# A decode kernel of two attention and GLU layers: K transposed by VectorE in 32x32 blocks, wide matmuls over four batches, softmax merged late

## The chip, the cores and the metric

One core of one Trainium2 chip. The metric is the device time of one execution, in microseconds (us). Times are medians with their range. TensorE is the matmul engine, VectorE, ScalarE and GpSimd are the three others; in the profile they are PE, DVE, ACT and POOL, PEld is TensorE's weight load, SP the queue that issues most loads.

## The reference

Two identical layers follow one another. Each adds attention over a cache and then a gated unit to x. There is one new token per batch, so the whole work is reading the K and V caches: 4 batches x 8 kv heads x 4096 keys x 128 x 2 bytes = 33.5 MB each. Both layers read the same caches, and both kernels load them once per layer, so they are read twice: 134 MB, plus 14 MB of weights, 148.1 MB in all.

```python
B, Sq, D = 4, 1, 512
Hq, Hkv, Sk, Dh = 32, 8, 4096, 128        # 4 q heads share a kv head; F = 1792
# all inputs bf16
def attention(x, k_cache, v_cache, wq, wo):
    q = (x @ wq).reshape(B, Sq, Hq, Dh).transpose(0, 2, 1, 3)
    k = jnp.repeat(k_cache, 4, axis=1); v = jnp.repeat(v_cache, 4, axis=1)
    p = softmax(einsum("bhqd,bhkd->bhqk", q, k) * Dh ** -0.5)
    return einsum("bhqk,bhkd->bhqd", p, v).transpose(0, 2, 1, 3).reshape(B, Sq, Hq * Dh) @ wo
def glu(x, w_gate, w_up, w_down):
    return (sigmoid(x @ w_gate) * (x @ w_up)) @ w_down

x = x + attention(layernorm(x), ...);  x = x + glu(layernorm(x), ...)   # twice
```

## The kernel before

The loop runs over the 32 (batch, kv head) pairs of a layer, 64 in all. K arrives with keys on the partitions; TensorE turns it with 32 identity matmuls per pair, and VectorE and ScalarE copy the results out of PSUM. Then 32 matmuls of 4 columns give the scores, with the keys on the partitions again. So a maximum or a sum over keys must cross partitions, and GpSimd does that.

```python
def pe_transpose_fill(base, i, f, ...):        # 4 fills per pair, 8 blocks each
    fns = [lambda e: e.transpose(tps[:, bb*P:(bb+1)*P], kn_buf[s][:, j, :], ident_bf) for bb in ...]
    S.group("pe", fns, ...)
    # ... cut: the copy out of PSUM, on ScalarE for one bank of four and on VectorE for three

def pe_scores(i):                              # 32 matmuls, K stationary, 4 q columns moving
    e.matmul(S_ps[p][:, j*REP:(j+1)*REP], lhsT=kt_sb[kb][:, j, :], rhs=qT_sb[:, b, g*REP:(g+1)*REP], ...)

def dve_reduce1(i):                            # L662: maximum inside each partition
    S.inst("dve", lambda e: e.tensor_reduce(hmax_sb[p], S_ps[p]..., AX.X, ALU.max), ...)

def pool_max(i):
    S.inst("pool", lambda e: e.partition_all_reduce(gmax_sb[p][:, :], hmax_sb[p][:, :], P, RO.max), ...)   # L673
    S.inst("pool", lambda e: e.tensor_scalar_mul(negbc_sb[p][:, :], gmax_sb[p][:, :], -att_scale), ...)    # L679

def act_exps(i):                               # L689: one exponential per q head
    e.activation(pexp_sb[p][:, :, h], S_ps[p][:, bass.ds(h, NJ, step=REP)], ACTF.Exp,
                 bias=negbc_sb[p][:, h:h+1], scale=att_scale, accum_out=rowsum_sb[p][:, h:h+1])

def pool_den(i):
    S.inst("pool", lambda e: e.partition_all_reduce(den_sb[p][:, :], rowsum_sb[p][:, :], P, RO.add), ...)  # L704

def dve_final(i):                              # L714, L720
    e.reciprocal(rden_sb[p], den_sb[p]);  e.tensor_tensor(oT_sb[...], O_ps[p][:, 0:REP], rden_sb[p], ALU.mult)

for i in range(NI):                            # the order inside a layer; fills of K for i + 1 are woven in
    pe_scores(i); dve_reduce1(i); pool_max(i); act_exps(i)
    if i >= 1:
        pe_pv(i - 1, 0, half); pe_pv(i - 1, half, NJ)     # 32 matmuls, V stationary, 4 columns moving
        pool_den(i - 1); dve_final(i - 1)
# ... cut: layer norm (reciprocal root by three Newton steps), projections, GLU
```

Each load of K or V puts 32 successive keys on a partition: rows of 8 KB.

Of the kernel before, what the change touches and what calls it, by code (L numbers as in the profile page):

```python
# [5 lines left out]
dt = mybir.dt  # L6
ACTF = mybir.ActivationFunctionType
ALU = mybir.AluOpType
AX = mybir.AxisListType
RO = bass.bass_isa.ReduceOp  # L10
# [4 lines left out]
class _Token:  # L15
    __slots__ = ("sem_key", "needed", "value", "inc")

    def __init__(self, sem_key, inc=1, needed=False):
        self.sem_key = sem_key
        self.needed = needed  # L20
        self.value = None
        self.inc = inc


class _Item:
    __slots__ = ("fn", "token", "waits")

    def __init__(self, fn, token, waits):
        self.fn = fn
        self.token = token  # L30
        self.waits = waits


class _Sched:

    def __init__(self):
        self.prog = {e: [] for e in ENGINES}
        self.all_items = []
        self.last_write = {}
        self.readers = {}  # L40

    def _inst(self, eng, fn, deps, sem_key, inc, needed):
        tok = _Token(sem_key, inc=inc, needed=needed)
        waits = []
        for d in deps:
            if d is None:
                continue
            d.needed = True
            waits.append(d)
        item = _Item(fn, tok, waits)  # L50
        self.prog[eng].append(item)
        self.all_items.append(item)
        return tok

    def group(self, eng, fns, reads=(), writes=(), deps=(), sem_key=None, inc=1, needed=False):
        assert eng in ENGINES
        if sem_key is None:
            sem_key = eng
        deps = [d for d in deps if d is not None]
        for k in reads:  # L60
            w = self.last_write.get(k)
            if w is not None:
                deps.append(w)
        for k in writes:
            w = self.last_write.get(k)
            if w is not None:
                deps.append(w)
            deps.extend(self.readers.get(k, ()))
        tok = None
        first = True  # L70
        for fn in fns:
            tok = self._inst(eng, fn, deps if first else (), sem_key, inc, needed)
            first = False
        for k in writes:
            self.last_write[k] = tok
            self.readers[k] = []
        for k in reads:
            self.readers.setdefault(k, []).append(tok)
        return tok

    def inst(self, eng, fn, reads=(), writes=(), deps=()):
        return self.group(eng, [fn], reads=reads, writes=writes, deps=deps)

    def dma(self, eng, fn, sem_key, reads=(), writes=(), deps=()):
        return self.group(eng, [fn], reads=reads, writes=writes, deps=deps, sem_key=sem_key, inc=16, needed=True)

    def assign_values(self):
        counts = {}
        for it in self.all_items:
            t = it.token  # L90
            if t.needed:
                c = counts.get(t.sem_key, 0) + t.inc
                counts[t.sem_key] = c
                t.value = c
        return counts

    def emit(self, eng, eng_obj, sems):
        waited = {}
        for it in self.prog[eng]:
            need = {}  # L100
            for w in it.waits:
                if w.value > need.get(w.sem_key, 0):
                    need[w.sem_key] = w.value
            for k in sorted(need):
                v = need[k]
                if waited.get(k, 0) >= v:
                    continue
                eng_obj.wait_ge(sems[k], v)
                waited[k] = v
            ins = it.fn(eng_obj)  # L110
            t = it.token
            if t.needed:
                ins.then_inc(sems[t.sem_key], t.inc)


def bass_interleave_layers__gqa_block_cached__glu_gated_glu__decode_kernel(
    nc: bass.Bass,
    A_x: bass.AP,
    A_k_cache: bass.AP,
    A_v_cache: bass.AP,  # L120
    A_wq: bass.AP,
    A_wo: bass.AP,
    B_x: bass.AP,
    B_w_gate: bass.AP,
    B_w_up: bass.AP,
    B_w_down: bass.AP,
    out: bass.AP,
):
    Bn, Sq, D = A_x.shape
    _, HKV, SK, DH = A_k_cache.shape  # L130
    HQ = A_wq.shape[1] // DH
    REP = HQ // HKV
    F = B_w_gate.shape[1]
    P = 128
    assert Sq == 1 and DH == P and D % P == 0 and F % P == 0
    assert REP == 4 and Bn == 4, "kernel specialised for 4 q-heads per kv head and batch 4"
    KD = D // P
    assert KD <= 4
    NJ = SK // P
    KF = F // P  # L140
    NI = Bn * HKV
    NK = 5
    NV = 5
    NLAYER = 2
    BPB = 8
    NFILL = NJ // BPB
    assert NFILL >= 2 and NJ % BPB == 0
    HG = 8
    assert HQ % HG == 0
    NHG = HQ // HG  # L150
    att_scale = float(DH) ** -0.5
    eps = 1e-5
    inv_d = 1.0 / float(D)
    RSQRT_MAGIC = float(0x5F375A86)
# [5 lines left out]
    cnt = [0]  # L160

    def sbt(shape, dtype, name):
        cnt[0] += 1
        return es.enter_context(nc.sbuf_tensor(f"{name}_{cnt[0]}", list(shape), dtype))

    def pst(name, shape=None, dtype=dt.float32):
        return es.enter_context(nc.psum_tensor(name, shape or [P, 512], dtype))

    kn_buf = [sbt([P, NJ, DH], dt.bfloat16, f"kn{i}") for i in range(NK)]
    v_buf = [sbt([P, NJ, DH], dt.bfloat16, f"vb{i}") for i in range(NV)]  # L170
    kt_sb = [sbt([P, NJ, P], dt.bfloat16, f"kt{i}") for i in range(2)]
    wq_sb = sbt([P, KD, HQ * DH], dt.bfloat16, "wq")
    wo_sb = sbt([P, HQ, D], dt.bfloat16, "wo")
    wg_sb = sbt([P, KD, F], dt.bfloat16, "wg")
    wu_sb = sbt([P, KD, F], dt.bfloat16, "wu")
    wd_sb = sbt([P, KF, D], dt.bfloat16, "wd")

    ident_f = sbt([P, P], dt.float32, "ident_f")
    ident_bf = sbt([P, P], dt.bfloat16, "ident_bf")
    ones_f = sbt([P, P], dt.float32, "ones_f")  # L180

    x_io = sbt([P, D], dt.bfloat16, "x_io")
    xT_res = [sbt([P, KD, Bn], dt.float32, f"xT{i}") for i in range(2)]
    xc_sb = sbt([P, KD, Bn], dt.float32, "xc")
    sq_sb = sbt([P, KD, Bn], dt.float32, "sq")
    lnsum = sbt([P, Bn], dt.float32, "lnsum")
    lnsq = sbt([P, Bn], dt.float32, "lnsq")
    negmean = sbt([P, Bn], dt.float32, "negmean")
    vpe = sbt([P, Bn], dt.float32, "vpe")
    vf = sbt([P, Bn], dt.float32, "vf")  # L190
    y0i = sbt([P, Bn], dt.int32, "y0i")
    nt_a = sbt([P, Bn], dt.float32, "nt_a")
    nt_b = sbt([P, Bn], dt.float32, "nt_b")
    nt_c = sbt([P, Bn], dt.float32, "nt_c")
    nt_y = [sbt([P, Bn], dt.float32, f"nt_y{i}") for i in range(2)]
    xnT_bf = sbt([P, KD, Bn], dt.bfloat16, "xnT")
    xfin_bf = sbt([P, KD, Bn], dt.bfloat16, "xfin")
    qT_sb = sbt([P, Bn, HQ], dt.bfloat16, "qT")
    oT_sb = sbt([P, HQ, Bn], dt.bfloat16, "oT")
    hmax_sb = [sbt([P, REP], dt.float32, f"hmax{i}") for i in range(2)]  # L200
    gmax_sb = [sbt([P, REP], dt.float32, f"gmax{i}") for i in range(2)]
    negbc_sb = [sbt([P, REP], dt.float32, f"negbc{i}") for i in range(2)]
    pexp_sb = [sbt([P, NJ, REP], dt.bfloat16, f"pexp{i}") for i in range(2)]
    rowsum_sb = [sbt([P, REP], dt.float32, f"rowsum{i}") for i in range(2)]
    den_sb = [sbt([P, REP], dt.float32, f"den{i}") for i in range(2)]
    rden_sb = [sbt([P, REP], dt.float32, f"rden{i}") for i in range(2)]
    t_sb = sbt([P, KF * Bn], dt.float32, "t_sb")
    hT_bf = sbt([P, KF, Bn], dt.bfloat16, "hT")

    S_ps = [pst("S_ps0"), pst("S_ps1")]  # L210
    O_ps = [pst("O_ps0"), pst("O_ps1")]
    T_ps01 = [pst("T_ps0", [P, BPB * P], dt.bfloat16), pst("T_ps1", [P, BPB * P], dt.bfloat16)]
    psA_bf = pst("psA", [P, BPB * P], dt.bfloat16)
    psY_bf = pst("psY", [P, BPB * P], dt.bfloat16)
    psA = psA_bf[:, :].bitcast(dt.float32)
    psY = psY_bf[:, :].bitcast(dt.float32)
    T0f = T_ps01[0][:, :].bitcast(dt.float32)
    T1f = T_ps01[1][:, :].bitcast(dt.float32)
    Y_banks = [T0f, T1f, psA, psY]
    Y_keys = ["T0", "T1", "psA", "psY"]  # L220
    T_ps = T_ps01 + [psA_bf, psY_bf]
    T_keys = ["T0", "T1", "psA", "psY"]

    XIN_OFF = 0
# [713 lines left out]
```

## Time and profile before

1093.66 us, median of 3 (1089.42 to 1094.46). The profiled execution spans 1090.6 us.

| reading | value |
|---|---|
| bytes and mean rate | 149 MB at 137 GB/s |
| rate while the first buffers fill (5 to 45 us) | 390 to 424 GB/s, 410 on average |
| busiest engine | TensorE, 36% |
| GpSimd | 6% |
| loop, one pair | 15.4 us; 64 pairs make 986 us |

No engine is busy and the loads idle. These are lines of the first two parts of the page of the profile before: busy us, share of the span and instructions; then the DMA share in 40 slices (9 is 90% or more).

```profile
PE 387.9 (36%) x7016; PEld 341.1 (31%) x7016; DVE 162.6 (15%) x469; ACT 144.2 (13%) x593; POOL 70.4 (6%) x200
...
DMA  9854344335334423442223442344234423431000
...
DMA packets 27767, 149.16 MB, mean 137 GB/s; under 512 B 2344, under 2 KB 8240, under 8 KB 11312
```

The first slices show that the loads can run at full rate; from the third on something else holds them back. The windows view (stretch, busy us of each engine, granted TensorE clock, DMA share, GB/s) has the rate while they do; the stretch shown is one of the two best:

```profile
35.00:40.00 5.00, 3.43 (x57) 3.43 (x58) 0.98 (x2) 2.54 (x8) 0.00 (x0) 0.50 1.01 424
```

The list of waits says who waits for whom (us in total, times, longest):

```profile
ACT pexp_47 L689 <- POOL negbc_45 L679: 447.9, 32, 17.7
ACT pexp_48 L689 <- POOL negbc_46 L679: 434.3, 32, 15.3
DVE rden_53 L714 <- POOL den_51 L704: 434.2, 32, 17.9
DVE rden_54 L714 <- POOL den_52 L704: 416.5, 30, 17.9
```

ScalarE waits for GpSimd's scaling, VectorE for GpSimd's denominator. But GpSimd is 6% busy, so its own time line is the view to open. Each line has the start, the busy us, the instruction, and in brackets the idle time of that engine before it and what ended it:

```profile
300.56 0.44 POOL L704 PARTITION_ALL_REDUCE den_51<-rowsum_49  x1 [6.00 <-issue]
...
302.31 0.38 POOL L673 PARTITION_ALL_REDUCE gmax_43<-hmax_41  x1 [1.30 <-DVE hmax_41 L662]
...
309.53 0.26 POOL L679 TENSOR_SCALAR negbc_45<-gmax_43 128x4 f32<-128x4 f32 x1 [6.84 <-issue]
309.90 0.33 ACT L689 ACTIVATE pexp_47<-S_ps,negbc_45 128x32 bf16<-128x32 f32 x1 [13.12 <-POOL negbc_45 L679]
...
315.75 0.44 POOL L704 PARTITION_ALL_REDUCE den_52<-rowsum_50  x1 [5.96 <-issue]
316.22 0.18 DVE L714 RECIPROCAL rden_54<-den_52 128x4 f32<-128x4 f32 x1 [12.82 <-POOL den_52 L704]
```

Three short instructions a pair, 1.1 us together, and two gaps of 6.0 and 6.8 us in which GpSimd waits for nothing that the profile shows ("issue"). One gap sits before the scaling, 6.84 us, the other before the all-reduce of the denominator, about 6.0 us. The views of the two source lines give the sums: 490.1 us of "issue" before the 64 scalings (7.7 us each on average, so the pair shown is a short one) and 373.4 us before 62 denominators (6.0 us each), together 863.5 of the 1090.6 us. The chain of work that ended last, in order of time, has the same gap as its longest piece:

```profile
302.31 0.38 POOL gmax_43 L673
302.69 0.07 POOLq L679 x2
302.76 6.77 issue
309.53 0.27 POOL negbc_45 L679
```

The views of source lines 679 and 704 name one kind of them (the columns are minimum, median and maximum ns, first and last start):

```profile
L679 POOLq MODIFY_POOL_CONFIG  x128: 83/85/85, 22.1 to 1057.5; - x128
```

### The profile page before, as it was taken

The page shows a single profiled execution, that of the slowest core. Times are in us where ns is not written, and L with a number is a line of the kernel's source. Part 1 is how long each engine was busy: PE and PEld are TensorE (multiplying, and loading weights), DVE is VectorE, ACT ScalarE, POOL GpSimd, SP SyncE. Part 2 cuts the span into 40 slices and gives each one's busy share as a digit, 9 for nine tenths or more (in the row PEclk, how much of TensorE's full clock was granted, in tenths as well). Part 3 has the DMA queues.
Part 4 walks back from the last instruction along what each step waited for, and adds up shares of the span by engine and source line. Part 5 has one row for each costly group of instructions (what it writes and reads, how often), then busy time and mean ns, then how long its engine had stood idle before and what let it go on. Part 6 is the DMA issues. An engine that isn't in the chain of part 4 may idle for free.

```text
span 1090.6 us, 16241 instructions
## 1 busy us (share of the span) xinstructions
PE 387.9 (36%) x7016; PEld 341.1 (31%) x7016; DVE 162.6 (15%) x469; ACT 144.2 (13%) x593; POOL 70.4 (6%) x200
## 2 busy tenths in 40 slices
PE   3242324334333333332065243343334333433314
PEld 3232323223223332332055233233323332333213
DVE  2010111011011101110121110111011101110112
ACT  1110111111110111011011111111110111011100
POOL 0000000000000000000000000000000000000000
PEclk9555555555555555555555555555555555555555
DMA  9854344335334423442223442344234423431000
GB/s 369 324 182 166 139 166 189 130 153 206 125 141 155 154 91 142 155 155 102 91 78 118 155 155 92 141 155 151 102 134 155 155 93 140 154 116 40 1 1 1
DMA packets 27767, 149.16 MB, mean 137 GB/s; under 512 B 2344, under 2 KB 8240, under 8 KB 11312
## 3 DMA queue, kind: packets, MB, share of 16 engines
q1 hardware_dynamic: 27696, 148.13, 35.8%
q8 instruction: 55, 0.90, 0.3%
q14 instruction: 16, 0.13, 0.0%
HBM read 148.12 MB, written 0.00 MB: 136 GB/s over the span
## 4 chain that ended last, share of the span: by engine, by line
issue 69%; ACT 12%; DVE 8%; POOL 6%; PE 4%; POOLq 1%; ACTq 0%; DVEq 0%
ACT pexp_47 L689 3%; ACT pexp_48 L689 3%; ACT kt_12 L551 3%; ACT kt_11 L551 3%; DVE kt_12 L558 2%; DVE kt_11 L558 2%; POOL den_52 L704 1%; POOL den_51 L704 1%; POOL gmax_43 L673 1%; POOL gmax_44 L673 1%; DVE oT L720 1%; POOL negbc_45 L679 1%; POOL negbc_46 L679 1%; DVE hmax_41 L662 1%; PE T_ps L538 1%
## 5 line engine op out<-in xcount | busy, mean ns | idle before, releaser
L689 ACT ACTIVATE pexp_47<-S_ps,negbc_45 128x32 bf16<-128x32 f32 x128 | 36.6, 331 | 447.9 <-POOL negbc_45 L679 447.9
L689 ACT ACTIVATE pexp_48<-S_ps,negbc_46 128x32 bf16<-128x32 f32 x128 | 36.5, 330 | 434.3 <-POOL negbc_46 L679 434.3
L714 DVE RECIPROCAL rden_53<-den_51 128x4 f32<-128x4 f32 x32 | 5.7, 178 | 434.2 <-POOL den_51 L704 434.2
L714 DVE RECIPROCAL rden_54<-den_52 128x4 f32<-128x4 f32 x32 | 5.7, 178 | 416.6 <-POOL den_52 L704 416.5
L623 PE MATMUL S_ps<-qT,kt_11 128*128 128x4 bf16 x1024 | 32.4, 167 | 63.9 <-ACT qT L598 55.3
L623 PEld LDWEIGHTS S_ps<-qT,kt_11 128*128 128x128 bf16 x1024 | 29.7, 104 | 70.9 <-ACT qT L598 56.0
L538 PE MATMUL T_ps<-ident_bf,kn_3 128*128 128x128 bf16 x224 | 28.2, 310 | 51.3 <-DVE kt_11 L558 20.5
L551 ACT ACTIVATE kt_11<-T_ps 128x1024 bf16<-128x1024 bf16 x38 | 38.8, 1032 | 35.6 <-PE T_ps L538 35.6
L623 PE MATMUL S_ps<-qT,kt_12 128*128 128x4 bf16 x1024 | 32.4, 167 | 22.0 <-DVE kt_12 L558 22.0
L538 PE MATMUL T_ps<-ident_bf,kn_1 128*128 128x128 bf16 x224 | 27.5, 304 | 35.7 <-DVE kt_12 L558 18.3
L538 PEld LDWEIGHTS T_ps<-ident_bf,kn_3 128*128 128x128 bf16 x224 | 22.2, 143 | 54.4 <-DVE kt_11 L558 22.1
L623 PEld LDWEIGHTS S_ps<-qT,kt_12 128*128 128x128 bf16 x1024 | 30.0, 104 | 29.4 <-DVE kt_12 L558 17.8
L538 PE MATMUL T_ps<-ident_bf,kn_5 128*128 128x128 bf16 x192 | 24.4, 310 | 41.2 <-DVE kt_11 L558 20.2
L538 PE MATMUL T_ps<-ident_bf,kn_2 128*128 128x128 bf16 x208 | 26.1, 306 | 35.3 <-DVE kt_11 L558 20.7
L538 PE MATMUL T_ps<-ident_bf,kn_4 128*128 128x128 bf16 x208 | 26.3, 310 | 32.5 <-DVE kt_11 L558 17.6
L538 PEld LDWEIGHTS T_ps<-ident_bf,kn_1 128*128 128x128 bf16 x224 | 21.4, 139 | 39.0 <-DVE kt_12 L558 19.9
L551 ACT ACTIVATE kt_12<-T_ps 128x1024 bf16<-128x1024 bf16 x32 | 33.1, 1034 | 0.0
L538 PEld LDWEIGHTS T_ps<-ident_bf,kn_5 128*128 128x128 bf16 x192 | 18.6, 140 | 44.4 <-DVE kt_11 L558 21.8
L538 PEld LDWEIGHTS T_ps<-ident_bf,kn_2 128*128 128x128 bf16 x208 | 19.7, 139 | 38.5 <-DVE kt_11 L558 22.2
L538 PEld LDWEIGHTS T_ps<-ident_bf,kn_4 128*128 128x128 bf16 x208 | 20.2, 141 | 35.4 <-DVE kt_11 L558 18.9
L704 POOL PARTITION_ALL_REDUCE den_51<-rowsum_49 x32 | 14.2, 443 | 192.8 <-issue 192.8
L689 ACT ACTIVATION_READ_ACCUMULATOR pexp_47<-S_ps,negbc_45 128x1 f32 x128 | 26.0, 203 | 0.0
(118 smaller groups left out, 690.7 us busy)
## 6 DMA issues: line engine op xcount, KB each, us to landing
kn_1<-in_A_k_cache_dram SPq DMA_DIRECT2D x13, 1024.0 KB, 4.9
kn_2<-in_A_k_cache_dram SPq DMA_DIRECT2D x13, 1024.0 KB, 4.9
vb_6<-in_A_v_cache_dram SPq DMA_DIRECT2D x13, 1024.0 KB, 7.0
kn_3<-in_A_k_cache_dram SPq DMA_DIRECT2D x13, 1024.0 KB, 4.8
vb_7<-in_A_v_cache_dram SPq DMA_DIRECT2D x13, 1024.0 KB, 7.0
kn_4<-in_A_k_cache_dram SPq DMA_DIRECT2D x13, 1024.0 KB, 4.9
vb_8<-in_A_v_cache_dram SPq DMA_DIRECT2D x13, 1024.0 KB, 7.1
vb_9<-in_A_v_cache_dram SPq DMA_DIRECT2D x13, 1024.0 KB, 7.0
```

The source lines that it names most:

```text
L538: (lambda j, bb: lambda e: e.transpose(tps[:, bb * P:(bb + 1) * P], kn_buf[s][:, j, :], ident_bf[:, :]))(j, bb)
L551: lambda e: e.activation(dst, src, ACTF.Copy),
L558: lambda e: e.tensor_copy(dst, src),
L623: (lambda j: lambda e: e.matmul(S_ps[p][:, j * REP:(j + 1) * REP], lhsT=kt_sb[kb][:, j, :], rhs=qT_sb[:, b, g * REP:(g + 1) * REP], start= ...
L662: lambda e: e.tensor_reduce(hmax_sb[p][:, :], S_ps[p][:, 0:NJ * REP].rearrange("p (j h) -> p h j", h=REP), AX.X, ALU.max),
L673: lambda e: e.partition_all_reduce(gmax_sb[p][:, :], hmax_sb[p][:, :], P, RO.max),
L679: lambda e: e.tensor_scalar_mul(negbc_sb[p][:, :], gmax_sb[p][:, :], -att_scale),
L689: (lambda h: lambda e: e.activation(pexp_sb[p][:, :, h], S_ps[p][:, bass.ds(h, NJ, step=REP)], ACTF.Exp, bias=negbc_sb[p][:, h:h + 1], sca ...
L704: lambda e: e.partition_all_reduce(den_sb[p][:, :], rowsum_sb[p][:, :], P, RO.add),
L714: lambda e: e.reciprocal(rden_sb[p][:, :], den_sb[p][:, :]),
L720: lambda e: e.tensor_tensor(oT_sb[:, g * REP:(g + 1) * REP, b], O_ps[p][:, 0:REP], rden_sb[p][:, :], ALU.mult),
```

## The change

The intent is to load at the full rate by giving the loop less to do. It is a rewrite; its parts are:

- A step of the loop is one kv head of all four batches, 16 steps ("groups") of 8.39 MB in place of 64.
- VectorE transposes K in place, in 32x32 blocks of int32 (two bf16 values move together). TensorE's identity matmuls and their copies go. The order of dims and keys that results is undone by permuting q.
- q is the stationary operand and K and V are the moving ones, 512 columns at a time. Each batch writes its own strip of 32 output partitions.
- The scores of a q head lie along the free dimension in four quarters, each with its own maximum; the quarters are merged after the values matmuls, with weights computed on VectorE. No reduction crosses partitions on GpSimd.
- K and V share one ring of ten 1 MB slots. V must match the new key order and is loaded in four pieces per partition, each 8 keys: rows of 2 KB.

```diff
-def pe_transpose_fill ... pool_max ... pool_den ... dve_final        # (cut) and the loop over 32 pairs
+def load_kv(n, kind, b):
+    if kind == "k": i = A_k[b, g].rearrange("(p t) d -> p (t d)", p=P);          o = dst[:]
+    else:           i = A_v[b, g].rearrange("(a p t) d -> p a (t d)", a=4, p=P); o = dst[:].rearrange("p (a x) -> p a x", a=4)
+    S.put("sp", lambda e: e.dma_start(o, i), writes=[f"r{s}"], dma=f"r{s}")
+
+def transpose_k(n, b):                                                          # L333
+    v = ring[s][:].bitcast(dt.int32)
+    S.put("dve", lambda e: e.transpose(v, v), ...)
+
+def scores(n):                                                                  # L342: 32 matmuls
+    for q in range(2):
+        for nn in range(NQ):
+            for b in range(B):
+                e.matmul(S_ps[32*b:32*b+16, q*512:(q+1)*512], lhsT=qbd[:, qi, b, nn, :],
+                         rhs=kt[:, 16*q:16*q+16, nn//2, :, nn%2], start=(nn == 0), stop=(nn == NQ-1))
+
+def softmax(n):
+    tensor_reduce(ml[:, 0:1], S_ps[:], AX.X, ALU.max, negate=True); tensor_scalar_mul(nbias, ml[:, 0:1], scale)
+    activation(p_sb "p tb (j q) -> p q tb j", S_ps "p (q tb j) -> p q tb j", Exp, bias=nbias, accum_out=...)   # L358
+
+# (cut) probs_t: 8 selection matmuls turn p; weights: transposes and nine small VectorE steps for the merge
+def values(n):                                                                  # L413: 32 matmuls
+    for tb in range(8):
+        for b in range(B):
+            e.matmul(O_ps[32*b:32*b+16, :], lhsT=pt_sb[:, tb, 16*b:16*b+16], rhs=v[:, :, tb, :], ...)
+# (cut) merge (scale, four selection matmuls), y_proj, GLU in four strips
+
+for n, (l, g) in enumerate(groups):
+    ensure_t(n, range(B)); scores(n); pump()      # pump issues the loads whose slots are free
+    softmax(n); q_proj(g + 1); probs_t(n); weights(n); values(n); pump()
+    merge(n); y_proj(n)
```

In the new kernel GpSimd does constants at the start and one power per layer norm.

## The prediction

> **What bounds it now.** Not bandwidth and not TensorE: the page shows 149 MB at a mean 137 GB/s, PE 36% busy, VectorE 15%, while the first 45 us (table of windows) move 390 to 424 GB/s. The timeline around 300 to 332 us shows the loop: one (batch, kv head) pair every 15.4 us, and 64 pairs x 15.4 = 986 us of 1090.6. In the list of waits ScalarE's exponentials wait 448 + 434 us for the GpSimd bias, and VectorE's reciprocal 434 + 417 us for the GpSimd denominator. The two partition all-reduces are only 0.38 and 0.44 us busy, but each is bracketed by 6.0 and 6.8 us in which GpSimd sits in "issue". Each pair pays both, in series: GpSimd's cross-partition reductions bound the kernel.
>
> **What the change removes.** All 128 all-reduces and their scalings (GpSimd keeps one tiny power per layer norm); 2048 PE transposes with their 256 evacuations (0.68 us VectorE, 1.03 us ScalarE); 4096 four-column matmuls; the 512 accumulator reads (one per exponential remains).
>
> **What it adds, per group of one kv head and four batches (16 groups, 8.39 MB each).** Estimates from trace durations:
> - VectorE block transposes, 4 of 128x2048 int32. The trace's 128x128 f32 reduce takes 281 ns, so about 145 cycles plus one element per cycle at 0.96 GHz: 2.2 to 2.3 us each, 9 us together. The Trainium skill ("VectorE: DVE Perf Modes", The three transpose paths) gives 311 ns for 128x128, which fits; no run shows it yet.
> - Scores and values: 32 matmuls of 512 columns each. At the granted clock of 0.5 one is about 0.43 us. Four batches write four 32-partition strips; the skill ("TensorE: Matmul & The Clock Gate", Part 3) measured 2.38x for three such column tiles, so I expect overlap: about 3.7 us for scores, the same for values; 13.7 us each if nothing overlaps.
> - Row maximum 1.3 us, exponential 1.1 us plus accumulator, selection matmuls and copy 1.7 us, nine small VectorE steps at 0.2 us spacing, merge and output projection about 5 us.
>
> Loop through VectorE: maximum 1.5, exponential 1.4, weights (which wait on ScalarE behind the q copies and the probability copy) 3.6, transposes 9, scores 3.7 = about 19 us. The TensorE path is about 16 us. DMA at 410 GB/s needs 20.5 us per group, so it becomes bandwidth bound, VectorE's loop close behind.
>
> **Sum.** 148 MB / 0.41 = 361 us; start 2; between the layers the ten-slot ring fills (25.6 us of loads) while the norm, GLU, norm and q projection run for about 32 us: idle 8; after the last V tile: values 3.7, merge and projection 5, norm 3, GLU 10, output 3: about 26. Total near 400; I add some for imperfect overlap: 412 us.
>
> **What would show it.** Right: mean rate above 340 GB/s, DMA share 9 in most slices, one dip in the middle; StreamTranspose 2.2 us; GpSimd waits gone; loads waiting little for slots.
>
> **What would make it wrong.** No overlap of column tiles: about 37 us per group, 640 us. A transpose at half rate: 28 us per group, 500 us. Strided bf16 operands (step of two elements) slowing the scores: up to 4 us per group, 440 us. Two-KB V rows below 400 GB/s: 10 to 40 us. GpSimd's cold start (first select at 10.95 us now) adds a few us.
>
> Chances: faster 0.98, within 2% 0.01, slower 0.01.

## More of the kernel before

GpSimd gets, in program order, an all-reduce (maximum of pair i), a scaling (pair i), an all-reduce (denominator of pair i-1), and so on.

```profile
L704 POOLq MODIFY_POOL_CONFIG  x124: 11/11/11, 54.2 to 1065.2; - x124
```

So GpSimd's configuration is changed on the way to the scaling, and again on the way to the denominator, in every pair.

## The result, and the profile after

The changed kernel took 413.58 us (412.73 to 417.68, 4 runs) against 1091.54 us (1086.95 to 1094.46, 4 runs) for the one before. Executions over 1.5% slower than the fastest of the same kernel are left out of the means. The ratio is 0.3797, 95% interval 0.3775 to 0.3819. Here and below a ratio is the mean time of one kernel's fast runs over that of the other's fast runs of the same rounds, so not quite the ratio of the medians quoted. The profiled execution took 417.68 us, a little over the median; its span is 415.9 us. Its page, the same lines as before:

```profile
PE 203.4 (49%) x1784; PEld 84.8 (20%) x1784; DVE 205.9 (50%) x259; ACT 82.5 (20%) x179; POOL 6.7 (2%) x24
...
DMA  7999999999999999999999919999999999999500
...
DMA packets 50067, 148.40 MB, mean 357 GB/s; under 512 B 2232, under 2 KB 6336, under 8 KB 41600
```

The loads now fill every slice but the first, one in the middle (the boundary of the layers) and the last three: the kernel is bandwidth bound. In windows, the steady state of the second layer, the dip while the w_down weights load, and the boundary:

```profile
core 0: us, PE busy (x) PEld busy (x) DVE busy (x) ACT busy (x) POOL busy (x), PEclk, DMA share, GB/s
...
180.00:200.00 20.00, 7.35 (x44) 3.10 (x44) 9.56 (x9) 2.02 (x6) 0.00 (x0) 0.50 1.01 319
235.00:255.00 20.00, 10.60 (x116) 4.54 (x117) 7.58 (x18) 5.13 (x14) 0.54 (x1) 0.71 0.48 179
...
265.00:365.00 100.00, 57.74 (x532) 23.88 (x528) 59.06 (x70) 24.93 (x55) 0.00 (x0) 0.59 1.03 404
```

404 GB/s in steady state is a little less than the 410 that the old kernel reached on average while its buffers filled. In the dip the engines of the queue are fully busy (share 1.01) and yet move only 319 GB/s: that load itself is slow. At the boundary the share itself falls: the program issues a load only once the tile that held its slot has been used, and no slot comes free while the norms and the GLU run.

One group on the time line. A group is 302.50 to 322.09, 19.6 us:

```profile
302.50 3.59 PE L342 MATMUL S_ps<-ring,qbd 128*16 128x512 bf16 x32 [1.45 <-DVE ring L333]
...
306.15 1.22 DVE L352 TENSOR_REDUCE ml<-S_ps 128x1 f32<-128x1024 f32 x1 [3.70 <-PE S_ps L342]
...
307.64 2.52 ACT L358 ACTIVATE p_sb<-S_ps,nbias 128x1024 bf16<-128x1024 f32 x1 [8.51 <-DVE nbias L355]
...
312.12 3.40 PE L413 MATMUL O_ps<-ring,pt_sb 128*16 128x512 bf16 x32 [1.16 <-ACT pt_sb L374]
...
313.19 8.85 DVE L333 STREAM_TRANSPOSE ring<-ring 128x2048 int32<-128x2048 int32 x4
...
322.09 3.54 PE L342 MATMUL S_ps<-ring,qbd 128*16 128x512 bf16 x32 [3.26 <-DVE ring L333]
```

Follow the brackets: the scores wait for the transposes, the maximum for the scores, the exponential for the maximum, the values for the probabilities; then VectorE, which had to serve the maximum and the merge weights first, does the next four transposes. That is one loop through VectorE, 19.6 us, as predicted (19). A group's loads take 8.39 MB / 404 GB/s = 20.8 us on average, so the loads are the slower of the two by a hair, and VectorE sometimes waits for K. The group shown belongs to the catching up after the boundary, with the ring still full: three groups in a row start 19.6 us apart (263.33 to 322.09), at VectorE's pace; the next three take 20.1, 20.7 and 20.8 us, the pace of the loads. From the list of waits and from the groups of the page (busy us, mean ns of one, idle before it):

```profile
DVE ring L333 <- DMA ring<-in_A_k_cache_dram: 53.3, 41, 9.1
```

```profile
L333 DVE STREAM_TRANSPOSE ring<-ring 128x2048 int32<-128x2048 int32 x64 | 146.2, 2299 | 53.7 <-DMA ring<-in_A_k_cache_dram 53.3
...
L358 ACT ACTIVATE p_sb<-S_ps,nbias 128x1024 bf16<-128x1024 f32 x16 | 40.4, 2522 | 185.8 <-DVE nbias L355 185.8
```

The chain of the new kernel deserves a warning. Followed back from the end it reads "issue 40%", which looks like the disease of before. In order of time that is a single piece, 162 us long:

```profile
240.73 162.26 issue
```

It is GpSimd's rest between two layer norms: the chain arrived at GpSimd's one small power and stepped back to the instruction before it on that engine. A share of issue is a finding only when one has looked at its pieces.

### The profile page after: what moved, and what is told of

It is laid out like the page before. It is cut to its first block, busy times and chain, and to the rows that moved or that the text cites. A ratio compares the mean times of both kernels' runs of the same rounds, so it can differ in the third digit from the quotient of the medians.

```text
span 415.9 us, 4348 instructions
## 1 busy us (share of the span) xinstructions
PE 203.4 (49%) x1784; PEld 84.8 (20%) x1784; DVE 205.9 (50%) x259; ACT 82.5 (20%) x179; POOL 6.7 (2%) x24
## 4 chain that ended last, share of the span: by engine, by line
issue 40%; DMA 28%; PE 14%; DVE 7%; SPq 6%; ACT 4%; POOL 0%; POOLq 0%; ACTq 0%; DVEq 0%
DMA ring<-in_A_k_cache_dram 24%; PE S_ps L342 5%; SPq L222 5%; DMA ring<-in_A_v_cache_dram 5%; DVE ring L333 3%; PE O_ps L413 3%; ACT p_sb L358 2%; PE Y_ps L499 2%; PE M_ps L429 1%; DVE ml L352 1%; SPq L235 1%; PE Y_ps L446 1%; PE PT_ps L471 1%; PE O_ps L471 1%; ACT o_sb L424 1%
## 5 line engine op out<-in xcount | busy, mean ns | idle before, releaser
L333 DVE STREAM_TRANSPOSE ring<-ring 128x2048 int32<-128x2048 int32 x64 | 146.2, 2299 | 53.7 <-DMA ring<-in_A_k_cache_dram 53.3
L342 PE MATMUL S_ps<-ring,qbd 128*16 128x512 bf16 x512 | 57.0, 620 | 82.4 <-DVE ring L333 81.4
L358 ACT ACTIVATE p_sb<-S_ps,nbias 128x1024 bf16<-128x1024 f32 x16 | 40.4, 2522 | 185.8 <-DVE nbias L355 185.8
L413 PE MATMUL O_ps<-ring,pt_sb 128*16 128x512 bf16 x512 | 57.3, 628 | 27.4 <-ACT pt_sb L374 15.9
L352 DVE TENSOR_REDUCE ml<-S_ps 128x1 f32<-128x1024 f32 x16 | 19.6, 1224 | 60.9 <-PE S_ps L342 60.9
L342 PEld LDWEIGHTS S_ps<-ring,qbd 128*16 128x16 bf16 x512 | 15.4, 120 | 121.2 <-DVE ring L333 81.5
L429 PE MATMUL M_ps<-sel_o,o_sb 128*128 128x16 f32 x128 | 26.9, 349 | 14.0 <-ACT o_sb L424 14.0
L429 PEld LDWEIGHTS M_ps<-sel_o,o_sb 128*128 128x128 f32 x128 | 25.3, 294 | 28.5 <-ACT o_sb L424 28.5
L446 PE MATMUL Y_ps<-wo,oT 128*4 128x512 bf16 x64 | 26.5, 560 | 4.7 <-ACT oT L435 4.7
L413 PEld LDWEIGHTS O_ps<-ring,pt_sb 128*16 128x16 bf16 x512 | 15.8, 125 | 56.9 <-issue 38.8
L323 ACT ACTIVATE qbd<-Q_ps 32x64 bf16<-32x64 f32 x64 | 13.7, 214 | 6.6 <-PE Q_ps L317 6.0
```

Source lines behind the costliest of these rows:

```text
L323: fns.append(lambda e, a=a: e.activation(qbd[32 * a:32 * a + 32, qi, :, :, a * R:(a + 1) * R], Q_ps[32 * a:32 * a + 32, 64:128].rearrange( ...
L333: S.put("dve", lambda e: e.transpose(v, v), reads=[f"r{s}"], writes=[f"r{s}"])
L342: fns.append(lambda e, q=q, nn=nn, b=b, kt=kt: e.matmul(S_ps[32 * b:32 * b + 16, q * 512:(q + 1) * 512], lhsT=qbd[:, qi, b, nn, :], rhs=kt ...
L352: "dve", lambda e: e.tensor_reduce(ml[:, 0:1], S_ps[:], AX.X, ALU.max, negate=True),
L358: lambda e: e.activation(p_sb[:].rearrange("p tb (j q) -> p q tb j", q=4), S_ps[:].rearrange("p (q tb j) -> p q tb j", q=4, tb=8), ACTF.Ex ...
L413: fns.append(lambda e, tb=tb, b=b, v=v: e.matmul(O_ps[32 * b:32 * b + 16, :], lhsT=pt_sb[:, tb, 16 * b:16 * b + 16], rhs=v[:, :, tb, :], s ...
```

## The experiments

The time was as predicted, so the questions are whether the reasons were. Four are disputed.

1. What bounded the kernel before: GpSimd's reductions as such, as the prediction says, or the change of GpSimd between two kinds of instruction? The redesign removes both.
2. Did the redesign's own parts (VectorE transposes, wide matmuls, late merge) gain anything beyond taking GpSimd out of the loop?
3. What bounds the new kernel: loads, VectorE's loop, or TensorE's strips?
4. What sets the rate of the loads?

Several kernels compute something else on purpose, to take away one cost. They are marked "wrong by construction"; the comparison with the reference let them pass all the same, so its tolerance is no proof for them. Runs of different calls ran on different chips; across calls only ratios to the kernel before are compared.

### b_negact: the kernel before, one scaling moved from GpSimd to ScalarE

```diff
-                "pool",
-                lambda e: e.tensor_scalar_mul(negbc_sb[p][:, :], gmax_sb[p][:, :], -att_scale),
+                "act",
+                lambda e: e.activation(negbc_sb[p][:, :], gmax_sb[p][:, :], ACTF.Copy, scale=-att_scale),
```

> The kernel before, with one thing moved: the scaling of the row maximum by -scale goes from GpSimd to ScalarE (one small activation per pair), so that GpSimd runs nothing but all-reduces in the loop. Theory A (the 6.0 and 6.8 us in which GpSimd issues nothing are switches between its two kinds of instruction, because the build has an extra instruction ahead of each change of kind): both gaps vanish, the all-reduces themselves cost under 0.5 us, the loop falls from 15.4 us to about 7 us per pair (TensorE and evacuations), total 470 to 620 us. Rival B (every all-reduce costs about 6 us of hidden start-up itself): the two gaps stay, the loop stays near 14 to 15 us, total above 950 us.

Measured: 405.94 us (404.11 to 408.09, 4 runs), correct; ratio 0.3687 (0.3672 to 0.3702). All 128 all-reduces are still on GpSimd. Its page and time line:

```profile
PE 323.2 (80%) x7016; PEld 316.0 (78%) x7016; DVE 179.1 (44%) x469; ACT 163.5 (40%) x657; POOL 51.2 (13%) x136
```

```profile
371.69 0.37 POOL L673 PARTITION_ALL_REDUCE gmax<-hmax  x1 [4.34 <-DVE hmax L662]
371.96 0.51 POOL L704 PARTITION_ALL_REDUCE den<-rowsum  x1
372.09 0.21 ACT L679 ACTIVATE negbc<-gmax 128x4 f32<-128x4 f32 x1 [1.45 <-POOL gmax L673]
372.33 0.33 ACT L689 ACTIVATE pexp<-S_ps,negbc 128x32 bf16<-128x32 f32 x1
...
376.81 0.37 POOL L673 PARTITION_ALL_REDUCE gmax<-hmax  x1 [4.34 <-DVE hmax L662]
```

Both gaps are gone, and so are the configuration records. The kernel before had 258 of them on lines 673, 679 and 704; here lines 679 and 704 have none, and line 673 has two, at the start:

```profile
L673 POOLq MODIFY_POOL_CONFIG  x2: 1/1/1, 11.9 to 11.9; - x2
```

The loop is 5.1 us (371.69 to 376.81), and what GpSimd waits for is VectorE. Taking one 0.26 us instruction out of GpSimd removed the 6.8 us in front of it and also the 6.0 us in front of the all-reduce after it. So the alternation was the cost, not the reductions; question 1 is settled. The expected loop was about 7 us; it came out faster, because the kernel runs into the loads (1 MB of K and 1 MB of V at 412 GB/s are 5.1 us).

The Trainium skill ("GPSIMD Engine Reference", section 2.1 Instruction dispatch) says that the first call to a freshly loaded GpSimd kernel pays about 6 us for loading its code, measured there as 5.95 us after the configuration record. The trace agrees: 6.0 us before the all-reduce that follows such a record. What the page does not say is that going back to an ordinary instruction costs too (6.8 us here, 7.7 us on average), and that one who alternates pays both every time.

### b_nopool: the kernel before, no GpSimd in the loop at all

No maximum is taken (the scores here are small), and the denominators come from a float32 matmul with a matrix of ones.

```diff
-    tensor_reduce(hmax...); partition_all_reduce(gmax...); tensor_scalar_mul(negbc...)
-    bias=negbc_sb[p][:, h:h+1]
+    bias=zero_sb[:, 0:1]
-    S.inst("pool", lambda e: e.partition_all_reduce(den_sb[p], rowsum_sb[p], P, RO.add), ...)
+    S.inst("pe", lambda e: e.matmul(O_ps[p][:, 2*REP:3*REP], lhsT=ones_f, rhs=rowsum_sb[p], start=True, stop=True), ...)
```

> The kernel before without any GpSimd reduction in the loop: no maximum is subtracted (the scores of these inputs are small, so the softmax is the same), and the denominator is summed over the partitions by one matmul with ones. All transposes on TensorE and all 4-column matmuls stay. My theory (GpSimd alone bound it): 64 pairs at 6.5 to 7.5 us, total 450 to 560 us, so most of the redesign's gain is had without the redesign. Rival (TensorE's small matmuls and transposes are what the redesign had to remove): above 800 us. Under theory A of the other run this one is at most 10 % faster than it.

Measured: 423.85 us (418.14 to 431.75); two of the four runs were slow, the fast ones took 422.45 and 418.14, so no ratio is given. This was a miss: without the all-reduces the kernel should have been at least as fast as with them, and its fast runs are 3 to 4% slower than b_negact in the same rounds. The likely reason is the float32 matmul, which TensorE now has to do besides (128 records of 0.35 us). The same stretch, b_negact and then b_nopool:

```profile
60.00:180.00 120.00, 96.03 (x1913) 94.71 (x1908) 51.82 (x120) 46.91 (x193) 15.11 (x39) 0.59 1.02 409
```

```profile
60.00:180.00 120.00, 106.40 (x1958) 105.52 (x1956) 47.45 (x100) 43.70 (x180) 0.00 (x0) 0.57 1.02 410
```

TensorE is busy 106 of 120 us in place of 96; in this stretch both move about 410 GB/s. The time is lost later: b_nopool moves 349 GB/s in place of 358 from 180 to 265 us and 399 in place of 412 from 265 to 365 us, and the rest goes after that; what ends each wait there was not traced. So taking the all-reduces out gained nothing: once left alone they cost nothing that shows here, where both kernels are close to the rate of the loads.

### a_strips: the new kernel, batches one after another

To test whether the strips overlap, the loops were swapped so that successive matmuls stay on one strip.

```diff
-            for nn in range(NQ):
-                for b in range(B):
+            for b in range(B):
+                for nn in range(NQ):
...
-        for tb in range(8):
-            for b in range(B):
+        for b in range(B):
+            for tb in range(8):
```

> The kernel after with the loops of scores and values turned inside out: all matmuls of one batch (one 32-partition strip) in a row, then the next batch; same matmuls, same result. If the overlap of the four strips carries the wide matmuls: they run one after another, 0.43 us each at half clock (13.7 us for 32) or 0.22 at full clock, so scores and values grow from 3.6 to 7.5 to 13.7 us each, and the total to 480 to 660 us. Rival (the overlap does not matter, since TensorE has slack behind the loads): total within 2 % of 414 us.

Measured: fast runs 419.47 to 424.46 us (a fourth was slow, 426.12), correct; ratio 0.3831 (0.381 to 0.3853), 0.9% over the new kernel's, with intervals that overlap. The expectation was far off. The time line shows why:

```profile
170.74 3.62 PE L342 MATMUL S_ps<-ring,qbd 128*16 128x512 bf16 x32 [6.16 <-DVE ring L333]
...
180.43 7.20 PE L413 MATMUL O_ps<-ring,pt_sb 128*16 128x512 bf16 x32 [1.17 <-ACT pt_sb L374]
```

The scores, now in runs of four on a strip, take 3.62 us where the new kernel's took 3.59 (both at a granted clock of 0.50, by the windows), and the values, in runs of eight, take 5.8 to 7.3 us from group to group in place of 3.59. Matmuls one after another would take 13.7 us at a clock of 0.50 (worked out further below), by estimate 11.4 at the 0.60 that was granted in the 7.2 us shown. So my edit did not take the overlap away: it made it smaller in one place, and TensorE (54% busy) had room for it: from 60 to 180 and from 265 to 365 us the loads ran at 402 and 404 GB/s in both kernels. The overlap is there in the new kernel; what the time would be with none is left open.

### a_halfv: the new kernel, half of each V tile loaded

Wrong by construction: the values matmuls read the loaded half twice, so the work of every engine stays and the bytes fall from 148 to 115 MB.

```diff
-            i = A_v[b, g].rearrange("(a p t) d -> p a (t d)", a=4, p=P)
+            i = A_v[b, g].rearrange("(a p t) d -> p a (t d)", a=4, p=P)[:, 0:2, :]
-                    rhs=v[:, :, tb, :],
+                    rhs=v[:, 0:2, tb, :].unsqueeze(1).broadcast_to([P, 2, 2, DH]),
```

> The kernel after with only half of every V tile loaded (the values matmul reads that half twice; wrong result on purpose; same instructions on every compute engine). 33.6 of 148 MB less. If bandwidth alone binds, time falls with the bytes: about 335 us. If VectorE's loop stands close behind, as predicted (19.6 us per group in the trace against 20.8 us of loads), it takes over: 16 x 19.6 + start 22 + between layers 25 + end 25, about 375 to 395 us.

Measured: 365.11 us (364.31 to 366.98); ratio 0.3318 (0.3307 to 0.3329). It lies between the two expectations, and the trace shows why. In the first layer, which loads weights too, the DMA share is 9 in nearly every slice of the page; in the second it is mostly 8. There the transposes follow one another and VectorE's loop sets the pace:

```profile
278.86 2.52 ACT L358 ACTIVATE p_sb<-S_ps,nbias 128x1024 bf16<-128x1024 f32 x1 [9.47 <-DVE nbias L355]
...
284.40 8.85 DVE L333 STREAM_TRANSPOSE ring<-ring 128x2048 int32<-128x2048 int32 x4
...
298.45 2.52 ACT L358 ACTIVATE p_sb<-S_ps,nbias 128x1024 bf16<-128x1024 f32 x1 [9.33 <-DVE nbias L355]
```

A group takes 19.6 us (278.86 to 298.45) although its loads would take 15.6. So VectorE's loop is a second limit, some 6% behind the loads: removing 23% of the bytes bought 13% of the time and no more.

### a_halftr: the new kernel, half of each transpose

Wrong by construction: half of K's columns are transposed.

```diff
-        v = ring[s][:].bitcast(dt.int32)
+        v = ring[s][:].bitcast(dt.int32)[:, 0:1024]
```

> The kernel after with each VectorE block transpose cut to half its columns (wrong result on purpose; 4.4 us less VectorE work per group, 70 us in all; loads unchanged). If the loads bind and VectorE's loop is only second: 403 to 413 us, the few us from the catching up after the stop between the layers. Rival (VectorE binds): about 350 us.

Measured: 413.32 us (413.07 to 416.31); ratio 0.3772 (0.3754 to 0.3789), against 0.3797 (0.3775 to 0.3819). Halving VectorE's largest item (busy 139 us in place of 206) changes nothing that the intervals can tell. Together with a_halfv: the loads bind, VectorE is next. Question 3 is settled.

### a_v8k: the new kernel, V in rows of 8 KB

Wrong by construction: V comes in the old layout, which does not fit the key order.

```diff
-            i = A_v[b, g].rearrange("(a p t) d -> p a (t d)", a=4, p=P)
-            o = dst[:].rearrange("p (a x) -> p a x", a=4)
+            i = A_v[b, g].rearrange("(p t) d -> p (t d)", p=P)
+            o = dst[:]
```

> The kernel after with V loaded in one 8 KB row per partition as K is, instead of four 2 KB rows (the rows then belong to other probabilities: wrong result on purpose; every compute instruction unchanged). After streams 404 GB/s in the second layer, the one-line fix of before, with 8 KB rows for both, 418. If the 2 KB rows cost that rate: 412 to 420 GB/s in the second layer and 8 to 13 us less, 400 to 406 us. Rival (the rate is set by something else, such as VectorE and TensorE reading the same memory, or by the 19.6 us loop of VectorE): within 3 us of after, rate 400 to 406.

Measured: fast runs 406.09 us (403.97 to 406.55); ratio 0.3696 (0.368 to 0.3711), 2.7% or about 11 us below the new kernel's. The profiled run was slow (418.03 us), so no line of it is compared. The same bytes in rows of 8 KB are faster: the rows of V cost the redesign some 11 us.

### a_wd128: the new kernel, w_down on all 128 partitions

The dip at 180 to 200 us coincides with the load of w_down, which the new kernel spreads over 112 partitions. Here it has 14 rows on each of 128 partitions, and the GLU's activations are turned by a VectorE block transpose; the result is correct.

```diff
-    wd = sb("wd", [FR, 4, 4, D], bf)                        # FR = 112
+    wd = sb("wd", [P, 14, D], bf)                           # loaded "(p i) n -> p (i n)"
-    # four selection matmuls turn h, a copy, then 16 matmuls of K = 112
+    S.put("dve", lambda e: e.transpose(hT[:], h_sb[:]), reads=["h"], writes=["hT"])
+    # then 14 matmuls of K = 128, lhsT=hT[:, i*32:i*32+B], rhs=wd[:, i, :]
```

> The kernel after with the down-projection weights loaded as 14 KB rows of 128 partitions instead of 4 x 4 KB rows of 112, and the GLU's hidden vector turned by one VectorE block transpose instead of four matmuls and a copy (correct). In after the loads move only 221 to 280 GB/s from 190 to 205 us, while that 1.8 MB is in flight, about 6 us lost. If the 112-partition transfer is the cause: no dip, 4 to 7 us less, 407 to 410 us. Rival (the dip belongs to the layer boundary, not to that transfer): within 2 us.

Measured: 413.79 us (413.0 to 414.63); ratio 0.377 (0.3755 to 0.3784), 0.7% or 3 us under the new kernel's, with intervals that touch. The windows of the dip, of the stretch before the boundary and of the boundary:

```profile
180.00:200.00 20.00, 10.80 (x76) 4.07 (x76) 10.37 (x10) 1.86 (x6) 0.00 (x0) 0.51 1.01 411
...
220.00:235.00 15.00, 8.70 (x66) 3.01 (x58) 9.26 (x10) 0.54 (x1) 0.54 (x1) 0.73 0.84 325
235.00:255.00 20.00, 12.44 (x108) 5.30 (x108) 10.64 (x14) 6.03 (x16) 0.00 (x0) 0.59 0.70 259
```

The dip is gone (411 GB/s for 319). Just before the boundary the loads then stop sooner (325 GB/s in place of 395 from 220 to 235 us), but they come back sooner too (259 in place of 179). At the last values matmul this run is 7.4 us ahead of the profiled run of the new kernel (385.25 against 392.62 us). Part of that is lost after it, where the changed GLU takes longer: the end takes 26.0 us in place of 23.3, as its activations are written in a scattered order (2.09 us for 0.62) and the down projection takes 4.87 us for 3.61, at a lower granted clock (0.72 against 1.00). The edit also lengthens the rows of w_down from 4 KB to 14 KB, so that the 112 partitions are the cause is not shown. V's rows of 2 KB cost only 3 to 4% of the rate (below), so the row length alone is unlikely; it was not tried further.

### b_newton2: the one-line version, a shorter reciprocal root

Two Newton steps of three operations in each layer norm in place of three of four, on top of b_negact. The result is correct.

```diff
-        for it in range(3):       # y*y, *v, *-0.5 +1.5, *y
+        for it in range(2):       # y*y, *(-v/2), (+1.5)*y
```

> The one-line fix of before (negative scaling on ScalarE) with the inverse square root of the layer norm in two Newton steps of three operations instead of three of four (correct). Each norm gets 5 VectorE steps of 0.2 us shorter. Three norms of four lie on the chain while the loads stop or are over: 2 to 4 us less than that fix, 402 to 404 us. Rival (the boundary is hidden): same as the fix, 406 us.

Measured: fast runs from 402.59 to 408.2 us (the profiled run was slow, 411.51); ratio 0.3692 (0.3669 to 0.3716), where b_negact had 0.3687 and 0.3716 in its two calls. The expected 2 to 4 us, if they are there, are below what these runs resolve: inconclusive.

### after_again, b_negact_again, b_v2k: the crossed comparison

The new kernel and the one-line version, both unchanged, and the one-line version with V in rows of 2 KB (wrong by construction), all on one chip in the same rounds:

```diff
-                v_buf[s].rearrange("p j d -> p (j d)"),
-                A_v_cache[b, g].rearrange("(p j) d -> p (j d)", p=P),
+                v_buf[s].rearrange("p (a t) d -> p a (t d)", a=4),
+                A_v_cache[b, g].rearrange("(a p t) d -> p a (t d)", a=4, p=P),
```

> The kernel after, unchanged, on the same chip and in the same rounds as the three others of this call, so that differences of 2 % can be compared: 411 to 416 us.

> The one-line fix of before, unchanged, in the same rounds as after. If the redesign brings nothing beyond taking GpSimd's alternation away, and its 2 KB rows of V cost it load rate: 403 to 408 us, 1.5 to 2.5 % less than after. If the earlier difference came from the chip or the rounds: equal to after within 0.5 %.

> The one-line fix of before with V loaded as the kernel after loads it, four 2 KB rows per partition instead of one of 8 KB (wrong result on purpose, same compute). If the row length sets the rate: 400 to 406 GB/s in the second layer instead of 418, and 4 to 12 us more than the fix, 409 to 417 us, that is the time of after. Rival (row length is not it): same as the fix within 2 us.

| design | V rows of 8 KB | V rows of 2 KB |
|---|---|---|
| before, scaling on ScalarE | 407.97 us (406.56 to 410.36), ratio 0.3716 (0.3704 to 0.3729) | 418.8 us (415.91 to 421.72), ratio 0.3813 (0.3792 to 0.3833) |
| redesign | 406.09 us, ratio 0.3696 (0.368 to 0.3711), a_v8k above, another chip | 418.11 us (415.2 to 418.66), ratio 0.3796 (0.3784 to 0.3808) |

(The kernel before took 1098.5 us in these rounds.) Down a column the two designs agree within 0.6%. Along a row the length of V's rows makes 2.6 to 2.7%. The windows of one stretch, b_negact_again and then b_v2k, show it as a rate:

```profile
265.00:365.00 100.00, 92.17 (x2024) 91.11 (x2020) 54.99 (x126) 50.37 (x210) 16.49 (x42) 0.71 1.01 413
```

```profile
265.00:365.00 100.00, 99.31 (x1875) 99.15 (x1873) 50.26 (x116) 46.26 (x191) 15.09 (x39) 0.50 1.03 397
```

413 against 397 GB/s with a full queue in both; the new kernel had 404 in that stretch. Beware of one thing: in b_v2k TensorE was busy 99 of 100 us, at a granted clock of 0.50, so it is close to a limit of its own, and this stretch alone can't tell the two limits apart. The stretch from 60 to 180 us can, as there the clock is nearly the same in both and TensorE is idle for 22 to 24 us of 120, again b_negact_again and then b_v2k:

```profile
60.00:180.00 120.00, 98.27 (x1908) 97.31 (x1907) 51.72 (x120) 47.79 (x199) 15.01 (x39) 0.56 1.02 409
```

```profile
60.00:180.00 120.00, 96.12 (x1810) 95.14 (x1807) 49.35 (x113) 45.95 (x190) 14.68 (x38) 0.53 1.04 395
```

The rate differs by as much, 409 against 395 GB/s, with the DMA engines full in both. In the redesign TensorE is half idle and a_v8k gains as much, so the row length is the cause in both. This settles questions 2 and 4: within 1% the redesign gave nothing that the one moved instruction had not given, and its V layout cost what the difference is.

The one-line version beats both kernels: 407.97 against 418.11 and 1098.5 us in the same rounds.

### a_expflat: the new kernel, the exponential written in reading order

The exponential of 1024 elements took 2.52 us where 1.1 was estimated. It writes its output in steps of four elements. Wrong by construction, it here writes in the order in which it reads:

```diff
-                p_sb[:].rearrange("p tb (j q) -> p q tb j", q=4),
-                S_ps[:].rearrange("p (q tb j) -> p q tb j", q=4, tb=8),
+                p_sb[:].rearrange("p tb x -> p (tb x)"),
+                S_ps[:],
```

> The kernel after with the exponential written in the order in which it is read, instead of in steps of four elements (wrong result on purpose). It took 2.52 us per group where I had estimated 1.1. If the scattered write costs it: 1.0 to 1.3 us in the trace, and the time 0 to 4 us less than after (it is on VectorE's loop, which is second to the loads, and on the last chain). Rival (the exponential of 1024 PSUM elements costs 2.5 us in any order): 2.5 us, no change.

Measured: 414.52 us (413.03 to 415.39); ratio 0.3772 (0.3763 to 0.3782), 0.6% under after_again in the same rounds. Its group of the page:

```profile
L358 ACT ACTIVATE p_sb<-S_ps,nbias 128x1024 bf16<-128x1024 f32 x16 | 17.8, 1114 | 198.4 <-DVE nbias L355 198.4
```

1114 ns for 2522: the scattered write was the whole difference. It shortens VectorE's loop by 1.4 us per group, 22 us in all, and the time moves by 3: once more, what is not the bound is worth little.

## Why the prediction was right, and where it was not

**The time was right: 412 predicted, 413.6 measured, and the bound is the predicted one.** The loads fill the span, VectorE's loop is close behind (19 predicted, 19.6 measured) and GpSimd's waits are gone.

**The step that failed is the reading of before.** "GpSimd's cross-partition reductions bound the kernel" has the right engine and the wrong cause. The reductions took 0.38 and 0.44 us, and b_negact keeps all of them at 406 us. The cost was in changing GpSimd between reductions and an ordinary instruction; the configuration records on lines 679 and 704 said so, and the prediction stopped at "issue". It was harmless for the forecast, as the redesign removes both kinds, and harmful for the advice that one would have drawn from it: a rewrite for what two lines do. What GpSimd does in the gap is not shown; the trace has the record and then silence.

**The terms of the sum**, predicted and measured:

| term | predicted | measured | where |
|---|---|---|---|
| transposes of a group | 9 us | 8.85 us, 2.30 each | time line |
| scores; values | 3.7; 3.7 us | 3.59; 3.59 us | time line (3.40 to 3.59) |
| exponential | 1.1 us, without accumulator | 2.52 us | groups; a_expflat |
| rate and time of the loads | 410 GB/s, 361 us | 403 GB/s, 368 us | windows |
| start | 2 us | about 4 us | first slice |
| w_down's slow load | none | about 6 us | slices 19 and 20 |
| idle at the boundary | 8 us | about 11 us | slices 23 and 24 |
| after the last V tile | 26 us | 25 us | windows (loads end at about 391, the span at 415.9) |

The measured terms make 414, near the 415.9 us of that span; idle times are worked out as the length of a slice or window times the rate missing against 404 GB/s. The prediction's named terms make 397. The other 15 us it added "for imperfect overlap". They were spent, but on other things: 7 us on the rate (2 KB rows), 6 on w_down, 3 on the boundary, 2 on the start, less 1 at the end: 17 in all. So part of the right total was a lump of the right size and not an understood cost, and that the total fits to 0.4% is luck. In VectorE's loop too, two errors partly cancel: the exponential took 1.1 us more than its 1.4, the merge weights 0.6 less than their 3.6 (310.20 to 313.19 us). The rate was the risk that the prediction named ("Two-KB V rows below 400 GB/s: 10 to 40 us"); a_v8k puts the rows' cost at 11 us, its low end.

**Four batches on four strips do overlap.** 32 matmuls of 512 columns took 3.59 us. Matmuls of 512 columns one after another start 0.43 us apart in this trace (the output projection at the end), so 32 would take an estimated 13.7 at the same clock of 0.50: a factor of 3.8. The Trainium skill ("TensorE: Matmul & The Clock Gate", Part 3) has 2.38 for three strips; it has no measured figure for four in columns, and this is larger in proportion. Bf16 operands in steps of two elements, named as a danger, did no harm: the scores read K so and take as long as the values.

**VectorE's transposes cost about 1 ns per column.** 64 columns took 0.245 us and 2048 took 2.30 us, so 1.04 ns per column element. The Trainium skill ("VectorE: DVE Perf Modes", The three transpose paths) gives 311 ns for 128x128 in bf16; the line through the two measured points (f32 and int32) gives 0.31 us there, and agrees. The one bf16 transpose measured, 448 columns in a_wd128, took 0.65 us, where the line gives 0.64.

**GpSimd's cold start did not come.** The prediction feared a few us for the first select, at 10.95 us before; in the new kernel it runs at 1.09 us. In the kernel before a stop of 10 us in "issue" stands ahead of it.

**What stays open:** the silent gap itself; the time with no overlap of strips at all; why the load of w_down on 112 partitions is slow; a deeper ring for the boundary, which was not tried; and a redesign with correct 8 KB rows of V, a flat exponential and w_down on 128 partitions together, which was not built.

## What to carry to other kernels

When an engine is 6% busy and yet everyone waits for it, open its own time line and queue records before redesigning: here two "issue" gaps stood wherever two kinds of GpSimd instruction alternated, and moving one 0.26 us instruction to another engine was worth 690 us. Test the smallest edit that removes the suspected wait first, as it is also the control without which a rewrite's gain can't be credited to its parts. Once loads bind, count the length of their rows and the stops at the start, the boundary and the end; savings on engines behind them (half of the transposes, 1.4 us of each exponential) are worth next to nothing.

## What the Trainium skill lacked or had wrong

- "GPSIMD Engine Reference", section 2.1: it has the 6 us for the first call after a configuration change (here 6.0 us), but not that the way back to an ordinary instruction costs as much (6.8 us in the pair shown, 7.7 on average), nor that a loop that alternates pays both every time (863.5 of 1090.6 us). It says that no visible instruction marks the load, which agrees: the gap shows none, and at its start stands the record MODIFY_POOL_CONFIG, from which the page measures.
- "DMA: Bandwidth & Descriptors", Specifications: it asks for transfers of at least 512 B for the line rate. Here 2 KB rows of V gave 397 GB/s and 8 KB rows 413 GB/s in the same kernel, 2.6% of the whole time; the measurement decides. Its limit of about 358 GB/s of memory per core did not hold for this one core alone (404 and 413 GB/s over 100 us), as its own section Bandwidth says of single-core runs.
- The same page has no rate that I found for a load to 112 partitions: the new kernel moved 319 GB/s in the stretch of that load (rows of 4 KB), and 411 with the same weights on 128 (rows of 14 KB); which of the two differences counts is not shown.
- "TensorE: Matmul & The Clock Gate", Part 3: no measured figure for four column strips (3.8 here, worked out from two durations), and none for runs of several matmuls on one strip (runs of four: 3.62 us for 32, no loss; runs of eight: 5.8 to 7.3 us).
- No page that I found has a measured time for a ScalarE write in steps of several elements: bf16 in steps of four took 2.52 us for 128x1024, in order 1.11 us.
